# Another order of the steps, and other places for the tiles, in a decay-attention and softplus feed-forward kernel

## The chip, the cores and the metric

The kernel runs on one core of a Trainium2 chip. The metric is the device time of one execution in microseconds; for the kernel before it is the median of three runs.

## What is computed

Attention with an exponential decay over blocks of 64 positions (4 batches, 8 heads, 768 positions, 64 dimensions), and behind it, on all 3072 tokens, a feed-forward of 512 to 2048 to 512 with a softplus between:

```python
for b in range(nb):                         # nb = 12 blocks of 64
    sl = slice(b * block, (b + 1) * block)
    qb, kb, vb = (q[:, :, sl], k[:, :, sl], v[:, :, sl])
    intra = np.einsum('bhic,bhjc->bhij', qb, kb) * Dmask[None]
    intra = np.einsum('bhij,bhjd->bhid', intra, vb)
    inter = np.einsum('bhid,bhde->bhie', qb * lam_pow[None], kv_state)
    out[:, :, sl] = intra + inter
    kb_dec = kb * rev_pow[None]
    kv_state = lam_block[None, :, None, None] * kv_state + np.einsum('bhsd,bhse->bhde', kb_dec, vb)
...
x = np.ascontiguousarray(attn_out.transpose(0, 2, 1, 3)).reshape(B * S, H * D)
h = x @ w_in
g = np.maximum(h, 0.0) + np.log1p(np.exp(-np.abs(h)))
return (g @ w_out).astype(np.float32)
```

## The kernel before

**Work.** The 768 positions are six chunks of 128, the 8 heads four pairs: 24 attention units g, of which g // 4 is the chunk. A unit's queries, keys and values are one tile `att<g>` of 1 MB, loaded in two halves of 512 KB; for the first four units the queries (`Lq`, 512 KB), keys (`Lk`, 256 KB) and values (`Lv`, 256 KB) come apart. On TensorE (PE) a unit is a block of small matmuls: scores and state sums (`x`, `y`, steps `x`, `y`, `xy`) and outputs (`z`). The weights come in 32 quarters and halves (`raw`, steps `L A0` to `L B15`).

**Feed-forward.** Each value is split into a high and a low part that PE takes at full speed, so a product is three matmuls of 128x512. Chunks 0 and 1 go plainly (`m`, `n` for the first layer into banks `h`; `l2`, `p2`, `e2`, `e3` for the second, into banks `o`; `fin`, `fn` store results over ACT's queue). Chunks 2 and 3 go together by seven products of half-size blocks in place of eight: `pr P1 i` to `pr P7 i` in the first layer for the eight slices i (L632), `o P1 i` to `o P7 i` in the second (L801). The block sums of weights that they need are made during the first chunks, sent to DRAM (`sA`, `sB`, `snd`, `sndB`: tiles `box`, `g1`, `g2`, `vP`), and read back: `w1 i` loads `w1a<i>` (1 MB) and `w1b<i>` (768 KB) for the first layer, `lv` loads a half `vP` of the second. Chunks 4 and 5 go the same way in code behind the list.

**Order.** Nothing reorders the program. One long string in the code is a list of some 1,200 steps; a loop looks each name up in `steps_of` and calls it, and each engine and each DMA queue does its part of the steps in exactly that order. All loads and scratch stores are issued from SP's queue (L127, L133, L167, L604, L605, L595 to L598); a load that waits for a tile's place holds back all loads behind it. ACT's queue does the same for its own work: `k g` (the decayed keys `kd`, L320) waits for the unit's second half, and casts and copies listed behind wait with it.

**Places.** Tiles of each size take numbered places in SBUF or PSUM from the tables `homes` ("b8": 21 places of 8 KB per partition; "b4", "b2", "bh" smaller; "o" four and "h" two PSUM banks), one entry per tile in the order in which they are made:

```python
at_ = {kind: iter(slots) for kind, slots in homes.items()}
```

**Banks of the second layer.** P1 and P2 share a pair of banks ("a"), P6, P7 and P4 another ("b"), P5 and P3 a third ("c"). Before P2 may go on in "a", `tk P1 0` and `tk P1 1` (L820, ACT) copy the sum of P1 out; P6 and P7 are taken by adds on DVE (L825).

Of the kernel before, what the change touches and what calls it, by code (L numbers as in the profile page):

```python
# [32 lines left out]
def decay_attention_softplus_ffn(  # L33
# [890 lines left out]
    for line in """  # L924
        scan 2, scan 3, scan 1, Lq 0, L A0, scale A0, round A0, x 0, Lq 1, Lv 0, scan 0, a 0, lpm, L A2, Lq 2, L A3,
        x 1, Lv 1, z 0, Lv 2, x 2, shift A0, mk64, lps, sign A0, rp1, add A0, a 1, hi A0, lo A0, lamc, yr 0, xh 0,
        xl 0, m 0 0, scale A2 A3, round A2 A3, a 2, z 1, yr 1, Lk 0, z 2, k 0, Lq 3, y 0, xh 1, yr 2, st 0, x 3,
        shift A2 A3, sign A2 A3, add A2 A3, xl 1, m 0 1, sum 1, L u4, k 4, Lv 3, a 3, xy 4, xh 2, z 3, hi A2 A3, xl 2,
        a 4, m 0 2, Lk 2, k 2, yr 3, xh 3, uh 4, ul 4, y 2, xl 3, m 0 3, q 4, z 4, L A1, scale A1, shift A1, lo A2 A3,
        sign A1, Lk 1, k 1, act 0, round A1, L u5, y 1, q 5, k 5, st 1, st 2, xy 5, L A4, m 3 1, add A1, a 5, m 3 2,  # L930
        uh 5, L A5, yr 4, T 0 0, ul 5, L u6, Lk 3, scale A4 A5, z 5, xh 4, yr 5, shift A4 A5, T 0 1, m 2 2, L u7,
        sign A4 A5, hi A1, k 6, lo A1, round A4 A5, m 3 3, add A4 A5, m 2 3, m 3 0, act 3, k 3, q 6, m 2 1, xh 5,
        m 2 0, xy 6, k 7, L B0, y 3, L B1, st 3, xl 4, L A6, act 2, xy 7, uh 6, Th P5 1, a 6, hi A4 A5, round B0 B1,
        z 6, yr 6, scale B0 B1, xl 5, a 7, m 1 1, uh 7, m 1 0, m 1 2, lo A4 A5, L B5, sum 2, m 5 1, shift B0 B1, m 1 3,
        act 1, ghi 1, m 5 3, m 5 0, xh 6, n 1 0, m 5 2, act 5, q 7, L B2, n 1 1, sign B0 B1, T 1 0, xl 6, add B0 B1,
        z 7, ul 7, ph 2, L A7, yr 7, n 1 2, T 1 1, xh 7, xl 7, hi B0 B1, n 3 2, n 3 1, n 1 3, T 2 0, ul 6, L B3, ghi 2,
        glo 2, n 3 3, sA 0, n 3 0, bct 1, lo B0 B1, n 0 1, scale B2 B3, n 0 0, L B4, shift B2 B3, scale A6 A7, glo 1,
        L A8, T 2 1, ghi 0, glo 0, n 0 3, bct 3, L B8, n 0 2, scale B4 B5, pl 2, shift B4 B5, sA 1, round B2 B3, L B9,
        L A10, n 4 3, bct 0, l2 1, n 4 2, shift A6 A7, sign B2 B3, round A6 A7, Th P5 0, sign A6 A7, add B2 B3,
        Th P6 0, l2 0, ghi 3, glo 3, L A11, hi B2 B3, n 4 0, n 4 1, n 2 3, sign B4 B5, L A9, T 3 1, round B8 B9,  # L940
        round B4 B5, n 2 2, sB 0, bct 4, n 2 1, lo B2 B3, add A6 A7, n 2 0, add B4 B5, snd 2, sum 3, hi A6 A7,
        lo A6 A7, l2 2, L B6, Tl P5 1, Th P6 1, bct 2, ph 3, round A8 A9, pl 3, n 5 2, n 5 1, n 5 3, Tl P6 0, ghi 5,
        scale B8 B9, glo 5, n 5 0, Th P4 1, Tl P6 1, bct 5, Tl P4 1, shift B8 B9, scale A8 A9, shift A8 A9, T 3 0,
        l2 3, L B7, scale B6 B7, sign A8 A9, m 4 2, hi B4 B5, Th P7 1, lo B4 B5, add A8 A9, sB 1, m 4 3, m 4 0, m 4 1,
        act 4, ghi 4, Th P7 0, sA 3, glo 4, qp P1 3, qk 3 0, shift B6 B7, L u8, snd 3, k 8, L B11, qp P2 3, qd 11 3,
        qp P6 3, Tl P7 0, qk 3 1, l2 4, Tl P5 0, q 8, sB 2, Tl P7 1, qp P7 3, sign B8 B9, qp P5 3, round B6 B7,
        Th P4 0, Tl P4 0, sum 4, hi A8 A9, qk 3 2, qd 22 3, qp P4 3, qs 21 3, lo A8 A9, qp P3 3, sA 2, add B8 B9, ph 4,
        sum 0, hi B8 B9, pl 4, qd 12 3, qs 11 3, ghi 6, sign B6 B7, qp P1 4, l2 5, add B6 B7, qk 4 0, scale A10 A11,
        ghi 7, glo 7, qp P6 4, qp P2 4, qd 11 4, L B10, shift A10 A11, sA 4, qk 4 1, qp P7 4, qp P5 4, hi B6 B7,
        round A10 A11, lo B8 B9, glo 6, qk 4 2, qd 22 4, lo B6 B7, qs 11 4, scale B10 B11, qp P4 4, qs 21 4,  # L950
        sign A10 A11, snd 4, qp P3 4, round B10 B11, L B15, qd 12 4, qs 12 4, ph 0, L A13, add A10 A11, sum 5, L A12,
        ghi 8, glo 8, l2 7, pl 0, round A12 A13, hi A10 A11, xy 8, sh 0, uh 8, ul 8, l2 6, scale A12 A13,
        shift A12 A13, L B14, l2 8, ghi 9, sB 3, L A14, lo A10 A11, qp P1 5, qs 12 3, a 8, qp P2 5, sign A12 A13, L u9,
        ph 5, qk 5 0, pl 5, qp P6 5, add A12 A13, shift B10 B11, qd 11 5, kv 8, z 8, sign B10 B11, add B10 B11, snd 0,
        qk 5 1, L A15, qp P7 5, hi A12 A13, lo A12 A13, qs 22 4, qk 5 2, qp P5 5, qd 22 5, hi B10 B11, round A14 A15,
        sB 4, glo 9, qp P4 5, sum 6, qp P3 5, qd 12 5, qs 11 5, qs 21 5, qp P1 6, ghi 11, glo 11, ph 6, pl 6, qk 6 0,
        lo B10 B11, snd 5, round B14 B15, qp P2 6, qp P6 6, scale A14 A15, l2 11, qk 6 1, qp P7 6, ph 1, k 9, qd 11 6,
        ghi 10, L B13, qs 11 6, qp P5 6, q 9, qk 6 2, qp P4 6, qs 21 6, shift A14 A15, sign A14 A15, pl 1, L B12,
        scale B12 B13, add A14 A15, sA 5, qd 22 6, qp P3 6, glo 10, sA 6, l2 10, sum 7, qd 12 6, sB 5, shift B12 B13,
        sign B12 B13, round B12 B13, kv 9, add B12 B13, scale B14 B15, xy 9, uh 9, a 9, snd 6, L u10, ul 9, hi A14 A15,  # L960
        hi B12 B13, l2 9, snd 1, k 10, xy 10, L2b 4, L u11, ghi 13, lo B12 B13, glo 13, a 10, sh 1, l2 13, lo A14 A15,
# [210 lines left out]
```

## Time and profile before

| | |
|---|---|
| median of three runs | 555.8 us |
| all three | 555.8, 553.63, 558.08 us |
| profiled execution | 558.21 us |
| its span | 556.4 us |
| granted TensorE clock, mean | 0.996 |

The profiled execution is of the length of the slowest of the three. Its time is the span and 1.8 us around it. Times of rows below are from the start of the span.

### The profile page before, as it was taken

How to read it: one execution, taken by the hardware profiler on the slowest of the kernel's cores; microseconds unless marked ns; L12 is line 12 of the kernel's file. 1: busy time of each engine (PE TensorE's matmuls, PEld its weight loads, DVE VectorE, ACT ScalarE, POOL GpSimd, SP SyncE). 2: the span in 40 equal slices, each digit the busy share in tenths (PEclk: the TensorE clock that was granted, in tenths of full speed). 3: DMA queues.
4: the chain of work that ended last, by engine and by line, in shares of the span. 5: the costliest groups of instructions: out<-in, count | busy, mean ns of one | idle time of the engine just before them, and what ended most of it. 6: DMA issues, size and time to landing. Idle time of an engine off the chain costs nothing. (4 is left out here: it accounts for less than half of the span.)

```text
span 556.4 us, 11672 instructions
## 1 busy us (share of the span) xinstructions
PE 542.8 (98%) x4795; PEld 443.8 (80%) x4795; DVE 419.7 (75%) x670; ACT 309.1 (56%) x515; POOL 0.4 (0%) x5
## 2 busy tenths in 40 slices
...
DMA  8999899999999999978998987256597346903711
GB/s 297 405 342 297 304 299 366 351 351 346 408 362 369 376 397 393 353 271 282 359 333 282 329 307 303 77 167 235 198 387 316 133 151 229 372 6 101 240 40 75
DMA packets 59783, 155.95 MB, mean 280 GB/s; under 512 B 4818, under 2 KB 27602, under 8 KB 53586
## 3 DMA queue, kind: packets, MB, share of 16 engines
...
q8 instruction: 38, 0.62, 0.4%
...
## 5 line engine op out<-in xcount | busy, mean ns | idle before, releaser
L487 PE MATMUL o<-w,g 128*128 128x512 f32 x384 | 91.7, 393 | 0.1
L487 PEld LDWEIGHTS o<-w,g 128*128 128x128 f32 x384 | 71.2, 188 | 15.7 <-DVE g L453 0.4
L801 PE MATMUL r2P<-sP,vP 128*128 128x512 f32 x336 | 77.9, 391 | 1.1 <-ACT post L820 0.8
L801 PE MATMUL r4P<-sP,vP 128*128 128x512 f32 (+1 forms) x348 | 76.9, 382 | 0.5 <-DVE post L1120 0.5
L801 PEld LDWEIGHTS r4P<-sP,vP 128*128 128x128 f32 x348 | 63.9, 188 | 13.4 <-DVE post L1120 0.7
L801 PEld LDWEIGHTS r2P<-sP,vP 128*128 128x128 f32 x336 | 62.7, 188 | 14.8 <-ACT post L820 0.9
L767 ACT CAST sP<-act 128x512 fp32r<-128x512 f32 x80 | 48.3, 619 | 31.1 <-DVE act L752 10.3
L643 DVE TENSOR_TENSOR sP<-act,sP 128x512 fp32r<-128x512 f32 x80 | 53.5, 686 | 14.4 <-ACT sP L767 14.2
L864 ACT ACTIVATE act<-act 128x512 f32<-128x512 f32 x48 | 29.9, 631 | 38.7 <-DVE act L870 17.7
L399 DVE SCALAR_TENSOR_TENSOR st<-st,lam_c,y 64x256 f32<-64x256 f32 x72 | 31.7, 480 | 15.7 <-PE y L370 14.7
L474 PE MATMUL h<-x,w 128*128 128x512 f32 x144 | 36.2, 398 | 0.3 <-issue 0.2
L767 ACT CAST sP<-tP 128x512 fp32r<-128x512 f32 x32 | 19.9, 621 | 28.6 <-DVE tP L762 18.9
L474 PEld LDWEIGHTS h<-x,w 128*128 128x128 f32 x144 | 26.3, 188 | 7.0 <-issue 0.6
L861 DVE TENSOR_TENSOR act<-b,ta 128x512 f32<-128x512 f32 x16 | 11.1, 691 | 26.7 <-PE b L632 26.6
L632 PE MATMUL x<-xc2P,w1a 128*128 128x512 f32 x96 | 26.0, 408 | 0.0
L370 PE MATMUL y<-att,kd 64*64 64x64 f32 x576 | 23.5, 221 | 1.6 <-ACT kd L320 1.2
L643 DVE TENSOR_TENSOR sP<-tP,sP 128x512 fp32r<-128x512 f32 x32 | 21.6, 685 | 4.1 <-ACT sP L767 4.1
L368 PEld LDWEIGHTS x<-att 64*64 64x64 f32 x640 | 21.3, 135 | 4.0 <-issue 2.8
L632 PE MATMUL a<-xc4P,w1a 128*128 128x512 f32 x96 | 24.4, 389 | 0.0
L632 PE MATMUL b<-xc4P,w1b 128*128 128x512 f32 x96 | 24.4, 389 | 0.0
L368 PE MATMUL x<-att 64*64 64x64 f32 x640 | 24.1, 221 | 0.2 <-issue 0.2
L320 ACT ACTIVATE kd<-att,rp 128x256 f32<-128x256 f32 x40 | 18.2, 503 | 11.0 <-DMA att<-in_att 8.9
...
## 6 DMA issues: line engine op xcount, KB each, us to landing
att<-in_att SPq DMA_DIRECT2D x44, 512.0 KB, 9.2
raw<-in_wts SPq DMA_DIRECT2D x32, 512.0 KB, 6.7
w1a<-g SPq DMA_DIRECT2D x16, 1024.0 KB, 6.9
vP<-vP SPq DMA_DIRECT2D x16, 1024.0 KB, 7.0
g<-w SPq DMA_DIRECT2D x24, 512.0 KB, 7.2
...
vP<-g SPq DMA_DIRECT2D x48, 256.0 KB, 5.4
g<-box SPq DMA_DIRECT2D x16, 512.0 KB, 6.5
```

The lines of the kernel that those rows point to most:

```text
L320: nc.scalar.activation(kd[:, :, t], kt_of(g)[:, :, t], AF.Copy, scale=ends[:, h : h + 1])
L368: nc.tensor.matmul(x[r, cols], lhsT=k[r, b, t], rhs=q[r, b, t], start=True, stop=True)
L370: nc.tensor.matmul(y[half(1 - s), cols], lhsT=kd[r, b, t], rhs=v[r, b, t], start=True, stop=True,)
L399: nc.vector.scalar_tensor_tensor(out=to[:, :, t], in0=of[:, :, t], scalar=lam_c[r, h : h + 1], in1=u[:, :, t], op0=ALU.mult, op1=ALU.add,)
L474: nc.tensor.matmul(to, lhsT=w[:, i, cs], rhs=x[:, j, :], start=not done and n == 0, stop=len(done) == NP - 1 and n == 2,)
L487: nc.tensor.matmul(outs[c, b], lhsT=g[:, i, b * 128 : (b + 1) * 128], rhs=w[:, j], start=k == 1 and n == 0, stop=k == NF and n == 2,)
L632: nc.tensor.matmul(to, lhsT=first_weights(c, name, i, k, p), rhs=x[:, j, p], start=start and p == 0 and m == 0, stop=p == 1 and m == 2, sk ...
L643: nc.vector.tensor_sub(out=g[:, 1], in0=l, in1=g[:, 0])
L767: nc.scalar.copy(out=g[:, 0], in_=of)
L801: nc.tensor.matmul(to[:, cols], lhsT=w[:, k, x, n * 128 : n * 128 + 128], rhs=g[:, y, cols], start=fresh and m == 0, stop=count == NF // 2 ...
L861: nc.vector.tensor_add(out=to, in0=firsts[bank_, i], in1=p1u2[i][:, 0])
L864: nc.scalar.activation(to, of, AF.Softplus)
```

## The change

All steps stay, with all their transfers; the string holds them in another order, up to where the code of chunks 4 and 5 begins (at 399.9 us of the span before). The tables `homes` have other numbers, so that the tiles fit in the new order. The core of the diff:

```diff
     homes = {
         "b8": [
-            1, 0, 2, 3, 4, 5, 6, 7, 8, 9, 10, 11, 12, 13, 14, 15, 16, 17, 18, 19, 20, 0, 2, 5, 6, 1, 7, 12, 15,
...
+            1, 0, 2, 3, 4, 5, 6, 7, 8, 9, 10, 11, 12, 13, 14, 15, 16, 17, 18, 19, 20, 0, 4, 3, 5, 1, 7, 11, 15,
...
     for line in """
-        scan 2, scan 3, scan 1, Lq 0, L A0, scale A0, round A0, x 0, Lq 1, Lv 0, scan 0, a 0, lpm, L A2, Lq 2, L A3,
...
-        xbh P6 0, sp 13, sndB 0, d3 0, p2 13, d3 1, xbh P7 1, ul 16, fn 0, z 16, w1 1, xbl P7 1, plB 3, xbl P5 1, d4 0,
...
-        th P1 7, tl P1 7, t2 2, o P1 7, t2 1, L u22, k 22, s12 0, s12 7, o P1 1, uh 21, s21 7, o P1 4, sndB 6, z 21,
-        tl P2 3, th P2 4, tk P1 1, xy 22, th P2 1, tk P1 0, o P2 3, tl P2 1, tl P2 4, s12 6, t3 6, th P2 6, tl P2 6,
...
+        scan 3, L A0, scan 1, scale A0, Lq 0, x 0, scan 0, scan 2, L A2, mk64, lpm, L A3, round A0, a 0, rp1, Lk 2,
...
+        fin 3, e2 1, fin 1, sh 0, kv 11, p2 7, a 11, z 11, k 12, q 12, xy 12, qs 12 6, sp 0, k 13, p2 5, p2 0 1,
+        p2 0 2, sh 12, sp 12, sh 6, p2 0 3, qs 12 5, uh 12, ul 12, sh 1, sp 1, p2 1, qs 22 6, p2 2, L2 7, sp 4, xr 11,
...
+        sumB 1, xbl P3 1, p2 12, w1 1, e3 2, fn 2, fn 0, k 17, sndB 4, kv 17, e3 3, uh 16, ul 16, d4 0, pr P1 1, c1 1,
...
+        L u22, k 22, th P1 5, o P1 4, tl P1 5, t3 0, o P1 0, lv P6 0, s22 6, t2 0, th P6 0, tl P6 0, th P2 2, s21 7,
+        th P2 7, o P1 5, o P6 0, tl P2 2, o P6 1, tk P1 0, tk P1 1, tl P2 4, t2 4, s22 7, z 21, t3 2, L u23, plB 6,
+        th P2 1, tl P2 1, xy 22, t2 3, tl P2 7, lv P2 0, o P2 1, o P2 0, e1 0, k 23, o P2 2, th P2 3, ts P5 1, kv 22,
...
```

Three places show what becomes of it.

SP's queue at the start of the program, before; `128x1024` of `att` are a unit's queries, `128x512` keys or values, `raw` weights:

```order
L133 DMA att0_135<-in_att 128x1024
L167 DMA raw0_137<-in_wts 128x1024
L133 DMA att1_152<-in_att 128x1024
L133 DMA att0_135<-in_att 128x512
L167 DMA raw1_163<-in_wts 128x1024
L133 DMA att2_165<-in_att 128x1024
L167 DMA raw1_163<-in_wts 128x1024
L133 DMA att1_152<-in_att 128x512
L133 DMA att2_165<-in_att 128x512
L133 DMA att0_135<-in_att 128x512
L133 DMA att3_250<-in_att 128x1024
```

The same place of SP's queue now:

```order
L167 DMA raw0_129<-in_wts 128x1024
L133 DMA att0_136<-in_att 128x1024
L167 DMA raw1_154<-in_wts 128x1024 x2
L133 DMA att2_166<-in_att 128x512
L133 DMA att0_136<-in_att 128x512
L133 DMA att1_181<-in_att 128x1024
L133 DMA att0_136<-in_att 128x512
L133 DMA att2_166<-in_att 128x1024
L133 DMA att1_181<-in_att 128x512
L133 DMA att2_166<-in_att 128x512
L133 DMA att3_245<-in_att 128x1024
```

The weights of all four quarters of the first slices and the keys of unit 2 went ahead of the queries of units 1 and 2; unit 3's queries stay eleventh.

SP's queue at the load of `w1a1`, before; `vP5` to `vP3` are the stores of block sums of slices 1 and 0 for the second layer, `g1` and `g2` the scratch that holds the first layer's:

```order
L127 DMA att18_2715<-in_att 128x1024 x2
L604 DMA w1a0_2746<-g1_0_98 128x2048
L605 DMA w1b0_2747<-g2_0_106 128x1536
L595 DMA vP5_122<-box1_1_2180 128x2x256
L595 DMA vP6_123<-box1_1_2180 128x2x256
L595 DMA vP7_124<-box1_1_2180 128x2x256
L595 DMA vP3_125<-box1_1_2180 128x2x256
L595 DMA vP5_122<-box1_0_2423 128x2x256
L595 DMA vP6_123<-box1_0_2423 128x2x256
L595 DMA vP7_124<-box1_0_2423 128x2x256
L595 DMA vP3_125<-box1_0_2423 128x2x256
L604 DMA w1a1_2836<-g1_1_99 128x2048
```

The same place now:

```order
L595 DMA vP3_125<-box1_0_2243 128x2x256
L565 DMA w2b_1_2618<-g3_1_115 128x2048
L127 DMA att18_2625<-in_att 128x1024 x2
L565 DMA w2b_7_2712<-g3_7_121 128x2048
L127 DMA att17_2740<-in_att 128x1024 x2
L604 DMA w1a1_2767<-g1_1_99 128x2048
```

The load `w1a1` stands behind a scratch read and the load of unit 17 in place of eight box stores.

PE where the second layer goes from P1 to P2 (banks `r2P1_0` and `r2P1_1` hold both), before; `z21` is the output block of unit 21, `x22` the scores of unit 22:

```order
L801 MATMUL r2P1_1_3779<-sP1_1_3831,vP1_0_3648 128x512 x3
L801 MATMUL r2P1_0_3775<-sP1_4_3770,vP1_1_3599 128x512 x3
L801 MATMUL r2P1_1_3779<-sP1_4_3770,vP1_1_3599 128x512 x3
L382 MATMUL z21_3881<-qd_21_3659,st_21_2992 64x64 x4
L386 MATMUL z21_3881<-a_21_3773,v_21_3834 64x64 x4
L382 MATMUL z21_3881<-qd_21_3659,st_21_2992 64x64 x4
```

The same place now:

```order
L801 MATMUL r2P1_0_3695<-sP1_5_3841,vP1_1_3624 128x512 x3
L801 MATMUL r2P1_1_3699<-sP1_5_3841,vP1_1_3624 128x512 x3
L801 MATMUL r2P6_0_3875<-sP6_0_3861,vP6_0_3857 128x512 x3
L801 MATMUL r2P6_1_3879<-sP6_0_3861,vP6_0_3857 128x512 x3
L801 MATMUL r2P6_0_3875<-sP6_1_3685,vP6_0_3857 128x512 x3
L801 MATMUL r2P6_1_3879<-sP6_1_3685,vP6_0_3857 128x512 x3
L382 MATMUL z21_3897<-qd_21_3671,st_21_3007 64x64 x4
L386 MATMUL z21_3897<-a_21_3786,v_21_3788 64x64 x4
```

Two slices of P6, in banks of their own, came between the last product of P1 and the block of unit 21.

## Rows read from the trace of the kernel before

**Rows 1.** the page: PE's busy time, DMA share in 40 slices

```profile
PE 542.8 (98%) x4795; PEld 443.8 (80%) x4795; DVE 419.7 (75%) x670; ACT 309.1 (56%) x515; POOL 0.4 (0%) x5
...
DMA  8999899999999999978998987256597346903711
```

**Rows 2.** all waits of PE: engine line, waited for; us, times, longest

```profile
PE c L632 <- DMA w1a<-g: 2.8, 1, 2.8
...
PE y L370 <- ACT kd L320: 1.2, 1, 1.2
...
PE r2P L801 <- DVE post L825: 0.3, 1, 0.3
```

**Rows 3.** timeline of PE around the longest wait

```profile
224.25 0.34 PE L382 MATMUL z<-qd,st 64*64 64x64 f32 x8
...
233.53 2.10 PE L632 MATMUL c<-xc2P,w1a 128*128 128x512 f32 x6 [2.81 <-DMA w1a<-g]
```

**Rows 4.** windows, start and after it: length, busy of engines, PEclk, DMA, GB/s

```profile
18.00:22.00 4.00, 2.75 (x69) 1.94 (x69) 3.11 (x8) 1.95 (x5) 0.00 (x0) 1.00 1.04 399
232.00:236.00 4.00, 2.47 (x8) 1.99 (x9) 2.18 (x4) 0.34 (x1) 0.00 (x0) 0.82 1.03 426
236.00:240.00 4.00, 4.00 (x15) 3.20 (x14) 0.00 (x0) 1.03 (x2) 0.00 (x0) 0.76 0.63 263
```

**Rows 5.** the load waited for: SP's timeline; KB, us to landing

```profile
224.50 0.93 SPq L604 DMA_DIRECT2D w1a<-g  x1
...
w1a<-g SPq DMA_DIRECT2D x1, 1024.0 KB, 9.0
```

**Rows 6.** timeline of ACT, 316 to 332 us

```profile
325.75 0.91 ACT L320 ACTIVATE kd<-att,rp 128x256 f32<-128x256 f32 x2 [4.46 <-DMA att<-in_att]
...
329.59 0.59 ACT L820 COPY post<-r2P 128x512 f32<-128x512 f32 x1
```

**Rows 7.** timeline of PE, 320 to 332 us

```profile
330.23 2.11 PE L801 MATMUL r2P<-sP,vP 128*128 128x512 f32 x8 [0.80 <-ACT post L820]
```

**Rows 8.** timeline of ACT to 45 us: start, us, ..., [idle before <-releaser]

```profile
6.75 0.67 ACT L258 ACTIVATE c<-raw 128x512 f32<-128x512 f32 x1 [2.93 <-DMA raw<-in_wts]
...
13.19 1.15 ACT L258 ACTIVATE c<-raw 128x1024 f32<-128x1024 f32 x1 [0.95 <-DMA raw<-in_wts]
...
20.36 0.91 ACT L320 ACTIVATE kd<-att,rp 128x256 f32<-128x256 f32 x2 [2.05 <-DMA att<-in_att]
```

**Rows 9.** timeline of PE to 40 us, same columns

```profile
20.92 0.27 PE L370 MATMUL y<-att,kd 64*64 64x64 f32 x1 [1.19 <-ACT kd L320]
...
23.31 0.96 PE L474 MATMUL h<-x,w 128*128 128x512 f32 x3
...
24.85 1.35 PE L474 MATMUL h<-x,w 128*128 128x512 f32 x3
26.39 0.34 PE L382 MATMUL z<-qd,st 64*64 64x64 f32 x8 [0.19 <-DVE qd L325]
```

**Rows 10.** a unit's second half: SP's timeline; KB, landing

```profile
166.03 0.33 SPq L127 DMA_DIRECT2D att<-in_att  x1
...
att<-in_att SPq DMA_DIRECT2D x1, 512.0 KB, 9.0
```

**Rows 11.** PE, then ACT, about 172 to 183 us

```profile
171.81 7.87 PE L487 MATMUL o<-w,g 128*128 128x512 f32 x34
...
174.55 0.62 ACT L639 CAST g<-lb 128x512 fp32r<-128x512 f32 x1
```

**Rows 12.** tile vP, one box store of SP: first and last start; landing

```profile
L595 SPq DMA_DIRECT2D vP<-box x1: 1437/1437/1437, 217.8 to 217.8; - x1
...
DMA to landing us min/median/max: 7.8/7.8/7.8
```

**Rows 13.** ACT's stores issued beside that load, 223.6 to 227.4 us

```profile
out_dram<-ob ACTq DMA_DIRECT2D x4, 256.0 KB, 9.2
```

**Rows 14.** tile w1a from 200 to 300 us: landing of its eight loads

```profile
DMA to landing us min/median/max: 4.8/6.9/9.0
```

More of the change, by code (lines that the diff above doesn't have):

```diff
@@ L924, in decay_attention_softplus_ffn @@
     for line in """
-        scan 2, scan 3, scan 1, Lq 0, L A0, scale A0, round A0, x 0, Lq 1, Lv 0, scan 0, a 0, lpm, L A2, Lq 2, L A3,
[L926 to L959, printed above, removed]
@@ new lines, in decay_attention_softplus_ffn @@
+        scale A2 A3, Lv 0, z 0, round A2 A3, Lq 1, shift A0, sign A0, add A0, hi A0, yr 0, xh 0, shift A2 A3,
+        sign A2 A3, add A2 A3, Lk 0, k 0, Lq 2, lo A0, x 1, a 1, x 2, a 2, y 0, k 2, st 0, Lv 1, hi A2 A3, Lv 2, xl 0,
+        Lq 3, z 1, yr 1, L u4, sum 1, x 3, lps, q 4, xh 1, xl 1, k 4, lamc, m 0 0, z 2, yr 2, xy 4, a 3, xh 2, a 4,
+        m 0 1, Lk 1, k 1, Lv 3, z 3, yr 3, y 1, st 1, uh 4, xh 3, xl 2, lo A2 A3, ul 4, L u5, m 0 2, xl 3, z 4, k 5,
+        L A1, q 5, scale A1, shift A1, L u6, q 6, y 2, st 2, yr 4, xh 4, xy 5, uh 5, L A4, sign A1, m 0 3, m 3 0, Lk 3,
@@ new lines, in decay_attention_softplus_ffn @@
+        m 3 2, m 3 3, xl 4, k 6, xy 6, a 5, z 5, ul 5, act 0, round A1, add A1, hi A1, uh 6, L A5, scale A4 A5, k 3,
+        m 3 1, m 2 1, ul 6, T 0 0, m 2 0, L u7, act 3, q 7, L B5, shift A4 A5, a 6, lo A1, k 7, yr 5, T 0 1, xh 5,
+        sign A4 A5, m 2 3, m 2 2, act 2, L A11, y 3, xy 7, a 7, round A4 A5, add A4 A5, L B3, z 6, yr 6, xl 5, L B1,
+        ghi 0, m 1 2, m 1 0, m 1 3, L B4, st 3, T 1 0, uh 7, L A8, L B0, ghi 2, hi A4 A5, lo A4 A5, m 1 1, sum 2,
+        n 1 1, n 1 0, xh 6, xl 6, L B2, L B8, act 1, z 7, sA 1, yr 7, xh 7, xl 7, m 5 1, m 5 0, scale B0 B1,
@@ new lines, in decay_attention_softplus_ffn @@
+        n 4 1, hi B2 B3, Th P7 0, l2 0, lo B2 B3, add A6 A7, pl 2, sum 3, round B8 B9, round B4 B5, L A9, n 5 2, sB 0,
+        scale A8 A9, shift A8 A9, Th P5 0, l2 3, hi A6 A7, sA 2, lo A6 A7, ghi 5, glo 5, ph 3, n 5 3, pl 3, sB 1,
+        sign A8 A9, n 5 1, bct 5, Th P6 1, n 4 2, n 4 3, add B4 B5, snd 2, l2 2, Tl P7 0, Th P5 1, snd 3, scale B8 B9,
+        bct 4, shift B8 B9, sA 3, Tl P5 0, L A13, m 4 3, hi B4 B5, lo B4 B5, Tl P6 0, round A8 A9, add A8 A9, m 4 0,
+        m 4 2, m 4 1, Th P4 1, Tl P6 1, act 4, ghi 4, qp P1 3, qk 3 0, glo 4, Tl P5 1, qp P2 3, Th P7 1, Tl P7 1,
@@ new lines, in decay_attention_softplus_ffn @@
+        hi A8 A9, lo A8 A9, sA 4, qp P6 3, qk 3 1, sB 2, qd 11 3, Th P4 0, L B10, scale B6 B7, l2 4, L u8, qp P7 3,
+        round B6 B7, qp P5 3, qk 3 2, shift B6 B7, Tl P4 0, Tl P4 1, qp P4 3, qs 21 3, L A12, sum 4, qd 22 3,
+        sign B6 B7, sign B8 B9, qp P3 3, qd 12 3, add B8 B9, ph 4, pl 4, qp P1 4, qk 4 0, add B6 B7, hi B8 B9,
+        lo B8 B9, ghi 7, l2 5, qp P6 4, qp P2 4, sum 0, qd 11 4, qk 4 1, scale A10 A11, hi B6 B7, L A14, shift A10 A11,
+        sign A10 A11, qp P7 4, L B11, kv 8, qp P5 4, qk 4 2, qd 22 4, qp P4 4, qp P3 4, qs 11 4, glo 7, sB 4, lo B6 B7,
@@ new lines, in decay_attention_softplus_ffn @@
+        l2 7, add A10 A11, qd 12 4, qs 11 3, ghi 6, ghi 8, glo 6, glo 8, l2 8, ph 0, q 8, L A15, sum 5, L B12, qs 21 4,
+        hi A10 A11, lo A10 A11, scale A12 A13, shift A12 A13, snd 4, ph 1, k 8, xy 8, a 8, uh 8, ul 8, round A12 A13,
+        ghi 9, glo 9, round A14 A15, sB 3, sign A12 A13, round B10 B11, L B13, l2 6, ph 5, sA 5, L u10, qp P1 5, pl 5,
+        qp P2 5, scale B10 B11, shift B10 B11, qk 5 0, qd 11 5, pl 0, snd 0, add A12 A13, sign B10 B11, snd 5, qp P6 5,
+        scale B12 B13, z 8, sum 6, qk 5 1, qp P7 5, qk 5 2, qp P5 5, qd 22 5, hi A12 A13, lo A12 A13, sA 6, qp P4 5,
```

112 lines of the change are left out of this document (59 added, 53 removed), and 44 rows, old and new, of the table homes.

## The prediction

> **What bounds the kernel now.** I read the page first: PE is busy for 542.8 of 556.4 us, 98% [rows 1], and the change takes no matmul away. So the question is only which of PE's waits go and which come. The list of PE's waits comes next [rows 2]: one long wait for the load `w1a`, 2.8 us; 1.2 us for `kd` of unit 4 in the start; 0.3 us for an add that takes P6's bank in the second layer. One of 0.8 us for a copy of P1's bank stands in the same list; its row comes below. Then the stretch around the longest: PE resumes at 233.53 after 2.81 us without work [rows 3], and the two windows behind it show a granted clock of 0.82 and 0.76 [rows 4], that is, part of each at the 1.2 GHz level and the rest at 2.4. What that costs: 4 us x 0.18 + 4 us x 0.24 = 1.7 us. The wait is thus worth 4.5 us. The load it waits for was issued at 224.50 and landed 9.0 us later, at 233.5 [rows 5]; PE was on time and the load was not. The 0.8 us wait at 330.23 [rows 7] has another origin: ACT stood 4.46 us in front of `kd` of unit 22 until 325.75 and reached the second copy of P1's bank only at 329.59 [rows 6].
>
> The ceiling follows at once. Behind the start, only 4.5 + 0.8 + 0.3 = 5.6 us of waits lie before the unchanged code; if all go and none come, the profiled execution of 558.2 us falls to 552.6, which is 1.0%.
>
> **The start: +1.0 us.** SP's queue is in order and the DMA engines are full there (the first slices of the DMA line are 8 or 9 [rows 1]), so a byte lands when the bytes ahead of it in the queue have. That gives a ruler from before: by the listed order, ACT's scaling of the first weights waited until 6.75 for the first 1024 KB, the next weights' until 13.19 for 3328 KB, and `kd` of unit 4 until 20.36 for 5632 KB [rows 8]: 2.80 us per 1000 KB first, then 3.11. In the new order unit 4 is complete at 5888 KB, since unit 2's keys come ahead of it: 256 KB x 3.11 = 0.8 us later, so its state sums start at 20.92 + 0.8 = 21.7 [rows 9]. From there to `z4` both orders hold the same work, two blocks of `h`, one `z`, one `y`; before it took 26.39 - 20.92 = 5.47 us, in which the last block of `h` stretched from 24.85 to 26.39, 1.5 us where its sibling takes 0.96 [rows 9]. In the new order the split that this block reads is made well ahead, so 0.6 us of it go: `z4` at 21.7 + 4.9 = 26.6, or 0.2 late. But ahead of unit 4 stands one block of `h` where there were two, so a block (0.9) is still owed: 1.1, taken as 1.0. Bounds: 0 (if the queries of units 1 to 3, at 3072, 3840 and 4864 KB, are all covered and the owed block later fills a gap) to +2.2 (if each of them also waits).
>
> **ACT in front of `p2 1`: +0.2 us.** `k 13` now stands ahead of the casts of slices 12, 6 and 1. Its unit's second half is at 57,344 KB of the queue; before, the bytes at that place were issued at 166.03 and landed 9.0 us later, at 175.0 [rows 10]. Behind it ACT needs some 3.3 us (two `kd`, three casts of 0.62 [rows 11] and a softplus): the high part is ready at about 178.3, the low part 0.7 later on DVE. PE reaches it, counted in matmuls done, at 178.8 of before, inside the row of 34 matmuls from 171.81 [rows 11], plus the 1.0 of the start. Nearly even: 0 to 1.7 us (the upper end when ACT's four result stores, 1 MB, delay the landing by 2.7), taken as 0.2.
>
> **The long wait: -4.5, and +0.5 for what replaces it.** `w1a1` was at byte 79.43 MB of SP's queue, in the new order at 77.33 MB: eight box stores are now behind it, a unit's load and a scratch read ahead. The store at that byte was issued at 217.8 and landed after 7.8 us, at 225.6 [rows 12]. But PE also comes earlier, for the product of slice 1 is now the first of all (`pr P1 1`); the same amount of matmul work had been done at 224.25 before [rows 3], and with 1.2 us of lag PE is there at 225.5. So the load lands just as it is wanted: 0.1 by the ruler, and more by the four stores of `fn` that ACT sends beside it (256 KB each, landing after 9.2 us [rows 13]). I take 0.5 us, without a fall of the clock: the window of the start that holds the 1.2 us wait has 1.00 [rows 4]. Bounds: 0, and the third rival's. Only the landing behind the queue counts here; the load by itself is quicker, eight of its kind took 4.8 us at least [rows 14].
>
> The row for that load is 9.0 us for 1 MB [rows 5]. The Trainium skill, page "DMA: Bandwidth & Descriptors", section "Anatomy of one DMA - SWDGE (gpsimd) path", fits one transfer as 2.0 us plus its bytes by 436 GB/s. By it 1 MB would take about 4.4 us (an estimate from that page), and the 0.5 above would be 0; the trace agrees with it only at its fastest load (4.8), where nothing was queued ahead, so the row decides.
>
> **The second layer: -0.15 us.** Between the last product of P1 and the first of P2 stood the blocks of units 21 and 22 alone; 12 matmuls of P6, 2.8 us at 0.23 each (34 in 7.87 [rows 11]), are now between as well, and `kd` of unit 22 is further ahead of the two copies on ACT. That removes the 0.8. Against it: between the last of P5 and the first of P3, in bank "c", only one slice of P4 (1.4 us) stands now, where three stood (4.1); the two adds there end no sooner than the same adds between P6 and P7, which had 1.4 us of cover too and left a wait of 0.3 [rows 2]. So a second wait of that size, 0.3 to 0.5. And one `vP` load for P3 has 5.7 us from place to use where it had 8.1: 0.2. Sum -0.8 + 0.45 + 0.2 = -0.15; from -0.8 (no new wait) to +2 (both double and P3's load is late).
>
> Moves without a price: attention blocks change neighbours among matmuls (one switch more), DVE is busy for 75% and ACT for 56% [rows 1], and the other loads move by less than their lead over use in the list of waits.
>
> **Sum.** +1.0 + 0.2 + 0.5 - 4.5 - 0.15 = -2.95: 555.2 us against the profiled 558.2. That execution is as slow as the slowest of the runs shown (553.63 to 558.08), and the long wait, which hangs on a landing, may have been shorter in the others; a gain that shrinks with it is 0 to 2.95 from the median, 552.8 to 555.8. I take the middle of 552.8 and 555.2: **554.0 us**.
>
> **Rivals.** *First, a clean run:* the start costs nothing, `w1a1` lands in time, no new wait comes in bank "c". 555.8 - 5.6 = 550.2 from the median, 552.6 from the profile. For it: the new waits are near zero by the ruler. Against: the 256 KB more ahead of unit 4 are certain. Chance 0.2.
>
> *Second, the order changes where PE waits and not how long:* the load gains 233.5 - 225.6 = 7.9 us, but its use moves ahead by 5.2 (from 233.53 - 2.81 = 230.7 [rows 3] to 225.5), the lag of the start keeps growing by the owed block's neighbours (+2.2), and both banks of the second layer wait (+2): +2.2 + 0.2 + 0.5 - 4.5 + 2 = +0.4, which is 556.2 from the median and 558.6 from the profile. Chance 0.2.
>
> *Third, slower:* ACT's `fn` stores share the DMA engines with `w1a1`, now in front of the very first product. Before, with four such stores out, it took 9.0 us to land where the fastest of its kind took 4.8 [rows 5, 13, 14]; the ruler holds that once, and would hold it too little if the stores now fall wholly into its flight. It decides from 227.5 on: a wait of 2.0 and a fall of the clock as before, 1.7, take the place of the 0.5, and the sum is +0.25. Landing at 229, it is 1.5 more: 559.9 from the profile, 557.5 from the median; with the start at its upper end too (+1.2), 561.1. Chance 0.15. The Trainium skill, page "DMA: Bandwidth & Descriptors", section "Queues, rings and completion order", says that each DMA engine takes its queues in turn, packet by packet; by that the stores take their full share of the engines and this rival, with its 559.9, is the likely case. The rows on the landing agree in direction and don't tell the share.
>
> That the list does not do what it says is excluded: the order on the engines is the list's.
>
> **How the numbers follow.** The forecast has 0.45 and lies between 552 and 556. The range holds it, the clean run but for its fastest part (549.5 leaves 0.7 us below 550.2 for the pieces of waits under 0.3 us), the second rival, and most of the third: 549.5 to 559.0. About 1% is what a measurement of this kernel tells from no change. Faster is under 550.2: half of the clean run, and 0.05 of the forecast if every run of before had the long wait: 0.15. Slower is over 561.4: the third rival's far end, and a load that nothing here shows late: 0.09. Within: 0.76.
>
> **What would show it.** In the new profile: PE's wait for `kd` of unit 4 ends at about 21.1 to 21.7; the first `pr` product starts at 225 to 226 with a wait of under 1.5 us for `w1a`, and no window behind it has a clock under 0.95; the wait for the copies of P1's bank is gone; a wait for DVE's `post` of about 0.3 us comes between P5 and P3. The forecast is wrong if a load that I hold to be covered (units 15, 17, 18, a half of `vP`) shows in the list of PE's waits with over 1 us, or if the clock falls anywhere else.

## The result, and the profile after

The new order is slower: 559.7 us (median of 14 runs, 557.75 to 561.11) against 555.68 (14 runs, 552.79 to 558.08), a ratio of 1.0073 with a 95% interval of 1.0054 to 1.0092. Forecast were 554.0 us, and 549.5 to 559.0.

The two profiled executions hide this: both took 558.2 us. Before's is slower than all its 14 timed runs, the new one's equals the third fastest of its 14. The mean clock that each run of before carries says why. Over 91 runs of before that stood beside the experiments, 50 had a mean clock of at least 0.999 and a median of 553.8 us, 41 had less and a median of 557.0. I read from this that the wait for `w1a` with its fall of the clock [rows 3, 4] is in somewhat less than half of before's executions; e5 below, which takes the wait out, bears it out. The new order has 12 of 14 runs at 0.999 or more, and is slower all the same: about 6 us slower than an execution of before without that wait.

PE's waits in the new profile, the answer to [rows 2] (waited for: us in total, times, longest):

```profile
PE z L357 <- DMA att<-in_att: 2.0, 1, 2.0
PE y L370 <- issue: 1.6, 2, 1.4
...
PE z L382 <- issue: 1.1, 1, 1.1
PE r2P L801 <- DVE sP L643: 0.9, 2, 0.6
PE o L487 <- issue: 0.9, 1, 0.9
PE r2P L801 <- DMA vP<-vP: 0.9, 1, 0.9
...
PE r2P L801 <- DVE act L867: 0.7, 1, 0.7
```

The load `w1a` is gone from the list. In its place stand several waits of about 1 us, and for three lines of the list the releaser is "issue": PE waited for nothing that the profile names. The longest, 2.0 us, is in the first loads at 10.62 us; with one of 0.9 at 13.86 it stands where before had three of 2.25 us in all. The load, PE's first product with it, and the windows behind, answering to [rows 5, 3, 4]:

```profile
217.18 0.33 SPq L604 DMA_DIRECT2D w1a<-g  x1
...
w1a<-g SPq DMA_DIRECT2D x1, 1024.0 KB, 7.2
...
225.22 1.07 PE L632 MATMUL x<-xc2P,w1a 128*128 128x512 f32 x4
...
228.00:232.00 4.00, 4.00 (x68) 3.37 (x59) 1.78 (x3) 2.67 (x5) 0.00 (x0) 1.00 1.03 360
232.00:236.00 4.00, 3.80 (x17) 2.82 (x15) 1.77 (x3) 2.25 (x5) 0.00 (x0) 1.00 0.93 337
```

The load landed at 217.18 + 7.2 = 224.4 and PE came to it at 225.22 without a wait; the clock stayed at 1.00. That is what the change had to gain, and it did.

The start, answering to [rows 8, 9]: unit 4's second half on SP's queue with its landing, then PE.

```profile
10.50 0.33 SPq L127 DMA_DIRECT2D att<-in_att  x1
...
att<-in_att SPq DMA_DIRECT2D x1, 512.0 KB, 8.4
...
24.35 0.34 PE L382 MATMUL z<-qd,st 64*64 64x64 f32 x8
...
28.00 0.21 PE L370 MATMUL y<-att,kd 64*64 64x64 f32 x1 [1.39 <-issue]
...
34.18 0.21 PE L382 MATMUL z<-qd,st 64*64 64x64 f32 x1 [1.09 <-issue]
```

Unit 4 was complete at 10.50 + 8.4 = 18.9, and its output block began at 24.35, two microseconds before its time in before (26.39 [rows 9]), though with one block of `h` (0.9 us) less done. Then PE stood twice, 1.39 us at 28.00 and 1.09 at 34.18, both times with "issue" as the releaser, and the lead was gone: PE's 627th matmul, ahead of which both kernels have done the same work, starts at 40.83 us, before at 40.51; the 1022nd at 104.39 in both.

The second layer (P1's last slices, then P3's first), with DVE ahead of the first wait, answering to [rows 6, 7]:

```profile
308.52 0.69 DVE L325 TENSOR_TENSOR qd<-att,lp 128x512 f32<-128x512 f32 x1 [1.40 <-DMA att<-in_att]
...
311.80 0.50 PE L801 MATMUL r2P<-sP,vP 128*128 128x512 f32 x1 [0.71 <-DVE act L867]
...
379.60 1.61 PE L801 MATMUL r2P<-sP,vP 128*128 128x512 f32 x6 [0.65 <-DVE sP L643]
382.10 2.09 PE L801 MATMUL r2P<-sP,vP 128*128 128x512 f32 x8 [0.89 <-DMA vP<-vP]
...
372.16 3.05 SPq L780 DMA_DIRECT2D vP<-vP  x2
...
vP<-vP SPq DMA_DIRECT2D x1, 1024.0 KB, 7.1
...
327.24 1.07 ACT L820 COPY post<-r2P 128x512 f32<-128x512 f32 x2
```

At 308.52 DVE ends 1.40 us of waiting for unit 21, whose load had been issued only at 302.0: `L u21, q 21` stand side by side in the list, and DVE takes its queue in order. The sums and splits of P1's last slices stand behind it, and PE waits 0.71 at 311.80. At 379.60 it waits for splits of P3, which stand on DVE behind the adds that take P5; at 382.10 for a half of `vP`, issued second of two loads at 374.9 and landing 7.1 us later. The copies of P1's bank (327.24) are on time; the wait of [rows 7] is gone.

The second layer as a whole, PE alone, between two places at which both kernels have done the same work to within one matmul (length, PE's busy time, matmuls, clock, DMA share, GB/s), first before, then now:

```profile
311.17:385.60 74.43, 73.31 (x687) 1.00 0.64 220
```

```profile
308.66:385.62 76.96, 74.41 (x688) 1.00 0.72 250
```

It takes 2.5 us more. By the same count the last slices of P1 (from 308.66) take 1.6 more, the step from P5 to P3 (from 374.23) 2.1 more, and the two stretches between them 1.2 less.

### The profile page after: what moved, and what is told of

Same layout as the page of the kernel before. It is cut to its first block, busy times and chain, and to the rows that moved or that the text cites. A ratio compares the mean times of both kernels' runs of the same rounds, so it can differ in the third digit from the quotient of the medians.

```text
span 556.4 us, 11659 instructions
## 1 busy us (share of the span) xinstructions
PE 541.7 (97%) x4795; PEld 442.3 (79%) x4795; DVE 419.9 (75%) x670; ACT 308.7 (55%) x515; POOL 0.4 (0%) x5
## 4 chain that ended last, share of the span: by engine, by line
PE 87%; DMA 5%; DVE 3%; ACT 2%; issue 1%; SPq 1%; ACTq 0%; DVEq 0%
PE o L487 16%; PE r4P L801 14%; PE r2P L801 12%; PE c L632 6%; PE h L474 6%; PE b L632 6%; PE x L632 5%; PE qx L632 5%; PE a L632 5%; PE x L368 3%; PE qc L632 2%; PE z L382 2%; PE z L386 2%; DMA out_dram<-ob 1%; DMA vP<-vP 1%; PE qa L632 1%
## 5 line engine op out<-in xcount | busy, mean ns | idle before, releaser
L368 PEld LDWEIGHTS x<-att 64*64 64x64 f32 x640 | 21.2, 135 | 4.3 <-issue 3.1
L632 PE MATMUL x<-xc2P,w1b 128*128 128x512 f32 x96 | 23.8, 392 | 0.4 <-ACT ta L873 0.4
L632 PE MATMUL x<-xc2P,w1a 128*128 128x512 f32 x96 | 24.0, 393 | 0.0
```

The source lines that it names most:

```text
L368: nc.tensor.matmul(x[r, cols], lhsT=k[r, b, t], rhs=q[r, b, t], start=True, stop=True)
L632: nc.tensor.matmul(to, lhsT=first_weights(c, name, i, k, p), rhs=x[:, j, p], start=start and p == 0 and m == 0, stop=p == 1 and m == 2, sk ...
```

## The experiments

The list of steps and the tables of places are all that differs in every kernel but the last. Where a part of one order is put into the other, the steps of a stretch are sorted as the other order has them, and the places follow.

**Parts of the new order in the kernel before, and back.** Four kernels, one cut each: e1 the first 138 steps, e2 steps 139 to 671, e3 all from step 767; e4 the new kernel with before's first 183.

```diff
 e1
-        scan 2, scan 3, scan 1, Lq 0, L A0, scale A0, round A0, x 0, Lq 1,
+        scan 3, L A0, scan 1, scale A0, Lq 0, x 0, scan 0, scan 2, L A2,
...
 e2
-        Th P5 1, a 6, hi A4 A5, round B0 B1, z 6, yr 6, scale B0 B1, xl 5, a 7,
+        ul 6, q 7, L B5, a 6, L A11, a 7, L B3, z 6, yr 6,
...
 e3
-        cu3 1, ul 17, kv 17, u3b 0, pr P4 0, xy 18, s21 0, z 17, xr 17,
+        kv 17, L2b 5, fullB 7, sndB 3, cu3 1, w1 2, pr P4 1, s21 1, pr P4 0,
...
 e4
-        scan 3, L A0, scan 1, scale A0, Lq 0, x 0, scan 0, scan 2, L A2,
+        scan 2, scan 3, scan 1, Lq 0, L A0, scale A0, round A0, x 0, Lq 1,
...
```

> The kernel before, with the steps of its first 30 us of PE work (up to the state sums of unit 7) in the new order and all later steps as before. Theory 'start': the new order of the first loads and attention blocks makes PE stop for want of instructions (1.6 and 1.3 us in the new profile, where the page names no releaser), so this kernel is slower by 1.5 to 3 us (ratio 1.003 to 1.005). Theory 'second layer': the start is worth nothing or a gain of up to 2 us, since unit 4's output block began 2 us earlier in the new profile; ratio 0.996 to 1.001.

> The kernel before, with the steps from 30 to 200 us of PE work in the new order, start and late part as before. Theory 'second layer': no difference beyond 1 us, ratio 0.998 to 1.002. Theory 'middle': the new order of unit loads, casts and first-chunk products costs 1 to 3 us even before the long wait is reached, ratio 1.002 to 1.005.

> The kernel before, with all steps behind 232 us of PE work (rest of the first layer of chunks 2 and 3, and their second layer) in the new order. Theory 'second layer': the new waits of 0.9, 0.5, 0.8 and 1.1 us for splits on DVE and for a half of vP come with it, in place of 0.4 and 0.5: slower by 2 to 4 us, ratio 1.004 to 1.007. Theories 'start' and 'middle': within 1 us, ratio 0.998 to 1.002.

> The new kernel, with the steps of its first 40 us of PE work in the order of before. Theory 'start': 1.5 to 3 us are given back, 557 us, ratio to before 1.002 to 1.004. Theory 'second layer': it stays at 559 to 560.5, ratio 1.006 to 1.009.

Measured, as medians and ratios to before: e1 560.2 us, 1.0107 (1.0070 to 1.0145); e2 573.9, 1.0346 (1.0309 to 1.0382); e3 567.8, 1.0241 (1.0200 to 1.0283); e4 562.2, 1.0134 (1.0089 to 1.0180). e2, e3 and e4 are slower than both parents, e1 is at least as slow as the new kernel, and all four lie above every time that was expected. So the sizes can't be read as shares: at each cut a load or a unit of the one order meets the other too late. Rows of PE, first of e2, then of e3 (the lines are one further down in these kernels):

```profile
PE c L633 <- DMA w1a<-g: 6.6, 1, 6.6
PE x L369 <- DMA att<-in_att: 5.2, 1, 5.2
```

```profile
PE x L633 <- DMA w1a<-g: 7.7, 1, 7.7
PE c L633 <- DMA w1a<-g: 2.4, 1, 2.4
...
PE r2P L802 <- DMA vP<-vP: 1.2, 2, 1.0
...
PE r2P L802 <- DVE act L868: 1.1, 1, 1.1
```

Two things carry over. The waits of the new second layer came along into e3 (1.1 us behind `act` on DVE, 1.2 for `vP`), and e1 has the "issue" waits of the new start at the same blocks, 1.0 us in state sums of unit 5 and 1.1 in the output block of unit 5.

**e5: before, with the load that PE waited for 1 MB earlier.** The one thing the change gains, by itself.

```diff
-        xbh P6 0, sp 13, sndB 0, d3 0, p2 13, d3 1, xbh P7 1, ul 16, fn 0, z 16, w1 1, xbl P7 1, plB 3, xbl P5 1, d4 0,
+        xbh P6 0, sp 13, w1 1, sndB 0, d3 0, p2 13, d3 1, xbh P7 1, ul 16, fn 0, z 16, xbl P7 1, plB 3, xbl P5 1, d4 0,
```

> The kernel before, with one step moved: the loads of w1a1 and w1b1 stand ahead of the four box stores of slice 0 (1 MB) in SP's queue, as in the new order they stand ahead of eight. Theory 'the long wait is there in most executions' (2.8 us and a fall of the clock in the profile, 2.5 in a second one): the load lands some 2.7 us earlier, and the kernel gains 1.5 to 3 us, ratio 0.995 to 0.997. Rival 'it is a rare event, so the new order had nothing to win there': within 0.7 us, ratio 0.999 to 1.001.

Measured: 553.1 us (552.22 to 554.82), ratio 0.9952 (0.9932 to 0.9973), all 11 runs at a mean clock of 0.999 or more. It is faster than both kernels, as its theory said. The long wait is worth 2.5 us of before's median, not the 4.5 of the profiled execution.

**e6 to e8, e13, e14: the new order mended.**

```diff
 e6
-        ..., y 2, st 2, yr 4, xh 4, xy 5, uh 5, L A4, sign A1, m 0 3, m 3 0, Lk 3, m 3 2, m 3 3, xl 4, k 6, xy 6, z 5
+        ..., y 2, st 2, yr 4, xh 4, m 0 3, xy 5, uh 5, L A4, sign A1, m 3 0, Lk 3, m 3 2, xl 4, k 6, xy 6, m 3 3, z 5
-        xy 16, kv 15, z 15, p2 9
+        xy 16, p2 9, kv 15, z 15
 e13, first part of e7
-        s21 6, L u21, q 21, tl P1 6, pr P3 6, k 21, t3 1, t2 1, th P6 1, pr P4 7, u2b 6, phB 6, o P1 6
+        s21 6, L u21, tl P1 6, pr P3 6, t3 1, t2 1, th P6 1, pr P4 7, u2b 6, phB 6, q 21, o P1 6, ..., o P1 2, k 21
 e14, second part of e7
-        tl P4 5, o P4 5, th P3 6, ts P4 4, ts P4 6, th P3 5, o P5 7, tk P5 0, tk P5 1, o P4 1, lv P3 0, o P3 1
+        tl P4 5, tl P4 2, th P3 6, ts P4 4, ts P4 6, th P3 5, o P5 7, o P4 5, tk P5 0, tk P5 1, o P4 1, o P4 2, lv P3 0, o P3 1
```

> The new kernel with three products moved between attention blocks: m 0 3 ahead of xy 5, m 3 3 between xy 6 and z 5, p2 9 between xy 16 and z 15. No load and no other step moves. Theory 'instruction supply' (PE runs through short instructions faster than the 16 KB packets of its instruction queue land, and goes on 1.2 to 1.6 us behind a landing): the three waits without a releaser (1.6, 1.3, 1.1 us in the new profile) shrink below 0.5 each, the kernel gains 1 to 3 us, 557 to 558.5 us. Rival 'these waits are for data that the profile does not name' (kd and masks of units 5 and 6, casts for p2): the waits stay at the same blocks and the time at 559 to 560.

> The new kernel with five steps moved in the second half: q 21 and k 21 behind the split sums that they held up on DVE and ACT, and o P4 5 and o P4 2 between the last product of P5 and the first of P3. Theory 'second layer': the waits of 0.9 (P1's splits behind the wait for unit 21), 0.8 (splits of P3 behind the adds that take P5) and 1.1 us (half of vP for P3) shrink to 0.7 in all, the kernel gains 1.5 to 2.5 us, 557 to 558.3 us. Rival 'these waits only take over time that another engine would ask for next': the waits move to the following products, time within 0.7 us of 559.7.

> The new kernel with the moves of both preceding kernels. If the two theories are right and independent, the gains add: 555 to 557 us, that is ratio 0.998 to 1.004 to the kernel before. If what delays PE is the loads and not the order of its work, the sum is less than 1.5 us.

> The new kernel with only the first of the two repairs of e7: q 21 and k 21 behind the split sums that wait behind them. The wait in the last slices of P1 took 0.9 to 1.4 us in six profiles of this order. Theory 'it is lost time': 558.2 to 558.9 us, 0.8 to 1.5 below the new kernel's 559.7, and the wait is not in the profile. Rival 'the delay is only handed on to the P3 stage': within 0.4 us of 559.7.

> The new kernel with only the second repair of e7: two slices of P4 between P5 and P3. The two waits there took 0.3 to 0.8 and 1.0 to 1.4 us in six profiles. Theory 'the half of vP comes late by a fixed amount': 1.0 us gained, 558.5 to 559, with 0.5 to 1 us of the wait for vP left. Rival 'no gain, since the earlier products of P4 come from the same total cover': 559.3 to 560.

Measured: e6 559.83 us (558.66 to 560.7), no gain; e7 557.75 (ratio 1.0034, 1.0010 to 1.0059); e8 558.16 (1.0048, 1.0027 to 1.0069); e13 558.06 (1.0063, 1.0032 to 1.0094); e14 558.54 (1.0061, 1.0035 to 1.0087). Against the new kernel, e7 gains 2.0 us by the medians and 1.8, give or take 0.8, by the means: the second layer's waits are lost time, and the rival, that they are only handed on, falls. The repairs apart are less sure: e14 gains 1.2 by the medians (by the means 0.8, give or take 0.7), e13 1.6 (1.0, give or take 1.1; its runs lie between 556.25 and 561.36), which noise could make. e8 is no faster than e7 and misses the sum that it was to show. What is left of them in e7, all of PE's waits between 300 and 390 us:

```profile
380.96 9.33 PE L801 MATMUL r2P<-sP,vP 128*128 128x512 f32 x40 [0.45 <-DMA vP<-vP]
```

e6 parts the blocks, against its theory without a gain, and changes only the place of the waits. In the start the one at 28.0 is gone and that at 34.11 is longer by 0.27; at 217.75 PE now stands inside the output block of unit 15, where in the new kernel it stood in a product:

```profile
34.11 0.21 PE L382 MATMUL z<-qd,st 64*64 64x64 f32 x1 [1.36 <-issue]
...
217.75 0.27 PE L386 MATMUL z<-a,v 64*64 64x64 f32 x2 [1.07 <-issue]
```

**e9 to e12: other cuts, and before's late part.** The cuts lie where both orders have done nearly the same steps: e9 the kernel of e5 with the first 301 steps in the new order, e10 the new kernel with before's first 301, e11 with before's steps 301 to 715, e12 with all of before's from 716.

```diff
 e9 (e10 the other way round)
-        scan 2, scan 3, scan 1, Lq 0, L A0, scale A0, round A0, x 0, Lq 1,
+        scan 3, L A0, scan 1, scale A0, Lq 0, x 0, scan 0, scan 2, L A2,
...
 e11
-        qp P2 3, Th P7 1, Tl P7 1, hi A8 A9, lo A8 A9, sA 4, qp P6 3, qk 3 1, sB 2,
+        Tl P4 1, scale B6 B7, Th P7 1, shift B6 B7, L u8, k 8, L B11, qp P2 3, qd 11 3,
...
 e12
-        kv 17, e3 3, uh 16, ul 16, d4 0, pr P1 1, c1 1, fn 3, xbh P2 1,
+        xbl P2 0, xbh P2 1, xbl P2 1, phB 1, e3 3, uh 16, a 16, plB 1, sndB 1,
...
```

> The kernel of e5 (before, w1 1 early: 553.1 us), with its first 70 us of PE work in the new order. The cut lies where both orders have done nearly the same steps. Theory 'start': the new order of the start costs 1 us or more by waits for instructions, 554 to 556 us. Rival 'the start is even, what it loses to instructions it had won from loads': 552.5 to 553.7 us.

> The new kernel (559.7 us), with its first 70 us of PE work in the order of before: the same part the other way round. Theory 'start': 557.5 to 558.7 us. Rival 'even': 559 to 560.3 us.

> The new kernel, with the steps from 70 to 215 us of PE work in the order of before (the load w1a1 back behind the box stores with them). Theory 'the middle costs by waits for instructions at the two attention blocks of units 16 and 15 (1.0 to 2.1 us in three profiles)': 1 us is won there, but the long wait for w1a1 returns in some executions, so 558 to 561 us and a wider spread. Rival 'the seam alone decides': above 562 us.

> The new kernel up to 215 us of PE work (its early w1a1 with it), and all steps of the list behind it in the order of before. Theory 'second layer': the 2 to 3 us of new waits for splits on DVE and for vP are gone, 556.5 to 557.8 us, as with the five moves of e7. If it comes below 555, the late part carries more than its waits show in the profiles; if it stays over 558.5, it carries less and the start or the middle carry the rest.

Measured: e9 557.56 us (554.71 to 561.28), e10 560.68 (555.98 to 563.07), e11 568.36, e12 562.94. All but e11, which fits its rival (the seam decides), came out above what their theories said. Again the cuts cost: e9 waits 1.41 us for a copy on ACT at its seam, e12 3.1 us for a state on DVE, and e11 3.7 us for a copy and 3.6 us for `w1a`, which is back behind the box stores.

```profile
87.37 0.96 PE L632 MATMUL qx<-xc0P,box 128*128 128x512 f32 x3 [1.41 <-ACT qa L696]
```

```profile
228.98 0.75 PE L382 MATMUL z<-qd,st 64*64 64x64 f32 x4 [3.11 <-DVE st L399]
```

So e9's +4.5 over e5 is not the price of the start, and taking the start back (e10) gained nothing. Both fit a start that is about even, and neither proves it; in the two profiled executions it is even (104.39 us for the same work, above).

**e15: the better kernel, with the copies of P1's bank earlier.**

```diff
-        z 21, tl P2 3, th P2 4, tk P1 1, xy 22, th P2 1, tk P1 0, o P2 3,
+        z 21, tk P1 1, tk P1 0, tl P2 3, th P2 4, xy 22, th P2 1, o P2 3,
```

> The kernel of e5 (before, w1 1 early: 553.1 us), with the two copies of P1's bank ahead of the casts that stood between them on ACT. In profiles with before's order the wait of P2 for these copies was 0.4 to 1.0 us, in that of e5 none. Theory 'it is there in most executions': 552.3 to 552.8 us. Rival 'gone with the earlier load': 553 to 553.5.

Measured: 555.17 us (552.26 to 555.78), ratio 0.9985 (0.9956 to 1.0014). Neither expectation held: 6 of its 11 runs took 555.2 to 555.8, which no run of e5 did. Its profile has two waits of 0.4 us in the second layer that e5's has not, for a split and for an add on DVE. e5 remains the best.

**e16: the load of unit 17 behind `w1 1`.**

```diff
-        xbl P6 1, L u17, xbh P3 1, ..., w1 1, e3 2, fn 2, fn 0, k 17, sndB 4, kv 17, ..., xy 17, plB 3, pr P1 0
+        xbl P6 1, xbh P3 1, ..., w1 1, L u17, e3 2, fn 2, fn 0, sndB 4, ..., k 17, xy 17, plB 3, pr P1 0, kv 17
```

> The new kernel with the load of unit 17 behind w1 1 in SP's queue, and its decayed keys and copied values later on ACT. Theory 'the packet with PE's next instructions lands late at 215 us because loads fill the DMA engines': the wait without a releaser there (1.0 to 2.1 us in seven profiles) falls below 0.5, w1a1 lands at least 1 us ahead of its use, 557.8 to 558.8 us. Rival 'the packet is requested late': the wait stays over 0.9, and the time at 559 or more.

Measured: 562.39 us, ratio 1.0130 (1.0088 to 1.0173). The wait at the fixed place is still there, so the load of unit 17 is not what delays the packet. That the packet is asked for late, as the rival has it, does not follow: the engines were as full as before (below, after e17). A second wait, of 1.94 us for the keys of unit 17, stands beside a median that is 2.7 us above the new kernel's:

```profile
217.73 1.53 PE L487 MATMUL o<-w,g 128*128 128x512 f32 x6 [1.05 <-issue]
...
231.00 0.27 PE L370 MATMUL y<-att,kd 64*64 64x64 f32 x1 [1.94 <-ACT kd L320]
```

**e17: the same work, 90 PE instructions later in the stream.** This kernel computes the same, with other warm-up matmuls.

```diff
-    keep_warm(WARM)
+    keep_warm(3); [nc.tensor.matmul(warm_ps[:, 0:8], lhsT=warm[:, :128], rhs=warm[:, 0:8], start=True, stop=True) for _ in range(48)]
```

> The new kernel, with three of the nine warm-up matmuls at the start replaced by 48 of 8 columns: 90 more PE instructions (a weight load and a matmul each) ahead of all the work, whose order and transfers stay. In ten profiles the waits without a releaser stand at the 690th, 944th, 1198th and 5010th PE instruction, whichever matmul that is. Theory 'instruction supply': they stay at those numbers, so they move 90 instructions (45 matmuls) ahead in the work, the one at 217 us out of the products and into the block of unit 15; sizes may change with the work that precedes. Rival 'data that the profile does not name': they stay at the same matmuls, 90 instructions later in the count. Time: 558.5 to 561 us by either.

Measured: 568.22 us, ratio 1.0248 (1.0216 to 1.0280): the small matmuls took 10.2 us, which delays the whole start and makes the time useless for the question. The places answer it. PE's waits without a releaser:

```profile
41.53 0.21 PE L368 MATMUL x<-att 64*64 64x64 f32 x1 [1.10 <-issue]
...
51.92 0.34 PE L386 MATMUL z<-a,att 64*64 64x64 f32 x8 [1.86 <-issue]
```

Counted in all of PE's rows of the trace, which are the weight loads, the matmuls and some 130 rows of semaphores and drains, the first stands at row 962 and the second at row 1474. (The count in the expectation leaves the 130 out: its 690, 944, 1198 and 5010 are rows 706, 962, 1219 and 5058.) In the new kernel the three stand at rows 706, 962 and 5058; in e6 and e8, where other work is there, at 962 and 5058; in e5 one at 1219. They are whole multiples of 256 apart, to within one row, and so are all 41 such waits of over 0.25 us in the 19 profiles, whatever work is there. In e17 nothing stands at 5058, and 0.7 us at 4802, which is 256 less. The rival's places, the same matmuls 90 rows later, have no wait: it falls.

The instruction queue moved 38 packets of 16 KB, one for every 256 of the 9,718 rows, and the trace has their starts. The packet that row 5058 needs started 2.9 to 3.9 us behind row 4802 in the ten profiles with the new order around it, and 0.9 to 1.6 us behind it in the seven with before's order there, which have no such wait. In e2, where the engines stood nearly idle from 206 to 210 us, it started at 211.8, 1.6 us ahead of row 4802, and in the quiet stretch from 430 to 500 us of the new kernel three packets started 39 to 43 rows ahead of such a place. What differs is how full the DMA engines were just before a packet's start: first e16 at 215.2, then the new kernel at the quiet 460.6 (length, PE, PEld, DVE, ACT, POOL, clock, DMA share, GB/s):

```profile
212.00:215.20 3.20, 3.20 (x134) 2.87 (x134) 2.44 (x5) 2.59 (x4) 0.00 (x0) 1.00 1.01 421
```

```profile
457.60:460.60 3.00, 3.00 (x15) 2.49 (x14) 2.05 (x3) 0.63 (x1) 0.00 (x0) 1.00 0.33 113
```

So that the packet stands behind loads, as the theory of e16 had it, is the better reading, though the load of unit 17 is not the one; its rival is the worse. Why the packet stands 1.3 to 3 us longer in the new order than in before's, at a share of about 1.0 in both, is not shown.

## Why the prediction was wrong

The terms stand beside what the two profiled executions show when PE's time is compared at places of the same work (to within one matmul, 0.23 us). The forecast from the profile was -2.95. The stretch of the long wait took 3.0 us less in all, which two rows split into -3.9 and +0.95.

| stretch, us of before | forecast | shown |
|---|---|---|
| start and `p2 1`, to 212.75 | +1.2 | +0.2 |
| long wait and what replaces it, to 274.92 | -4.0 | -3.9 |
| wait at row 5058, in the same stretch | not on the list | +0.95 |
| rest of the first layer, to 311.17 | 0 | +0.3 |
| second layer, to 385.60 | -0.15 | +2.5 |
| sum | -2.95 | 0.0 |

**The long wait.** Right in its mechanism: `w1a1` landed at 224.4 (forecast 225.6) and PE came at 225.2 (225.5), with no fall of the clock. Wrong in its size for the median: I priced it at 4.5 us, from the slowest execution of before, and took half of the difference to the median off at the end; e5 measures 2.5. That the new profile is one of the shortest executions of its kernel (558.2 for a median of 559.7) could not be foreseen. A reading beside it was wrong, and no term hangs on it: the load of 4.8 us [rows 14] went out at 239.35, while `w1b`, issued at 233.0 and landing 7.9 us later, was still under way; so it is not one with nothing queued ahead.

**The second layer, forecast at -0.15, is the step that failed.** The 0.8 us wait for the copies went, as said. But the list of moves "without a price" held that loads move by less than their lead over use. `q 21` had been put directly behind its own load, and DVE stood in front of it for 1.4 us; the last slices of P1 took 1.6 us more. Between P5 and P3 I looked for a wait in bank "c" of 0.45 and for 0.2 on `vP`. The place was right and the waits are larger, 2.1 us more for the same work: splits behind the adds, 0.65, and the half of `vP`, 0.89, since I took its landing from two loads of before that were issued 5.5 us apart (4.9 to 5.8 us) and here the two go out 2.7 us apart, the second landing after 7.1. e14 gives back 1.2 us of this by the medians, e7 2.0 of both. The sum of this term should have been about +2.5.

**The start, forecast at +1.0.** The ruler by bytes failed: unit 4 was complete at 18.9, not 21.2; in the window from 10 to 20 us the new order moved 404 GB/s where before moved 385. What was so won, some 1.1 us when the owed block of `h` is taken off, went to waits that I did not have: PE without instructions. Net it is +0.3 at 41 us and nothing at 104; e9 and e10 could not measure it.

**ACT in front of `p2 1`, +0.2:** no wait of PE shows there; within its bounds.

**What was not on the list at all** are the "issue" waits. The one at row 5058 is 0.75 to 1.96 us in ten profiles with the new order around it and in none of those with before's. Its cause, the supply of PE's instructions, is shown by its fixed place in the count of rows; that the packets come late because they stand behind loads is read from their starts, and no run tested it by emptying the engines there. e6 and e8 show that parting the blocks by one product does not cure it. Before's order has such a wait too, at row 1219: 0.33 us in its profile, 1.35 in that of e5.

**The rivals.** The third, slower by the stores of `fn`, had the sign and not the cause: `w1a1` was on time beside them. The second (556.2 from the median, 558.6 from the profile) comes nearest, at a chance of 0.2: its second layer at +2 was right, its start at +2.2 was not, so its nearness is in part luck.

**What stays open.** e7 at 557.75 and e5 at 553.1 still differ by 4.65 us. The wait at row 5058 explains some 1 to 1.5 of it, the start's rest 0.7 at most. The profiled executions of these two differ by 1.1 us only (555.92 and 554.82, the fastest and the slowest of their runs), so the rest lies in what differs between executions of the new order, which no single profile shows. One hint: the profile of e6 (560.70, the slowest of its runs) is 2.4 us behind the new kernel's at the end of the list, and 1.6 of that arise between 204 and 242 us, where PE waits 0.5 us for `w1a` and 0.7 for an operand from DVE that the new kernel's profile does not wait for. That the loads of the new order come late more often is likely and not shown.
